# A planned order that knows of a port VectorE and GpSimd share, with new ranks and costs, and two buffers swapped in the last stage

## The chip, the cores and the metric

The kernel runs on one core of a Trainium2 chip. Its time is the device time of one execution in microseconds (us). Before the change three runs took 959.69, 960.66 and 961.48 us; the median, 960.66, is the number that counts. The engines are called by their short names: PE is TensorE, DVE is VectorE, ACT is ScalarE, POOL is GpSimd, SP is SyncE, which here issues nearly all DMAs.

## What is computed

The reference is causal attention with a decay, followed by two gated layers:

```python
cum = np.cumsum(np.log(np.clip(f, 0.0001, 1.0)), axis=-1)
scores = np.matmul(q, k.transpose(0, 1, 3, 2)) / sqrt(64) + (cum[..., :, None] - cum[..., None, :])
attn = softmax(where(causal, -1e9, scores))            # 4 batches, 8 heads, 576 tokens, head size 64
x = (attn @ v), heads laid side by side                # 2304 tokens x 512
h = x @ w_in                                           # 512 -> 2048
x = (h * sigmoid(h)) @ w_out                           # 2048 -> 512
out = ((x @ w_a) * (x @ w_b)) @ w_out2                 # 512 -> 1536 -> 512
```

## The kernel before

The work runs in five stages, one behind the other on PE, with their edges interleaved. (1) Attention, in 16 pairs of heads: scores `s` into PSUM (L453), on DVE a scaled copy that also gives the row minimum (L479), on ACT the exponential with a row sum (L487), on PE transposes of the weights `p` into the banks `t_x` and `t_y` (L529), copies of those to SBUF as `th` (L534, on ACT or DVE), and the product with `v` into `pv` (L575). (2) The first gated layer into 2048 columns (`job`, L729 for the products). (3) Its way out (`out_first`, L935). (4) The second gated layer into 1536 (`job` again). (5) Its way out (`out_pairs`, L1083).

The matrix products of stages 2 to 5 are done with seven products instead of eight per 2 x 2 block, so sums and differences of quarters have to be formed first (`combine`), and every fp32 operand is split in two parts, `hi` (a cast on ACT, L619) and `lo` (value minus `hi`, L620), so that three matmuls stand for one. The `lo` part and the sums run on DVE or POOL. `either` lets the planner choose between the two, `ss` fixes DVE, `pool` fixes POOL. `make_forms` makes the seven forms of the activations (`x`, `xa`, `xb`), `load_unit` those of a unit of weights (`w`), from words that `decode` unpacks (on ACT L679 and L680, on DVE L681 and L682). Buffers go in turns: the weights of unit n lie in `wA`, `wB` or `wC`, by n modulo 3, and what a later stage puts there waits for the last product that reads the unit.

The order on every engine is not written by hand. Each piece of work is handed to `Plan.add` with an engine, a cost in ns, what it reads and writes and a rank (`prio`, lower first). `Plan.order` plays the pieces through with those costs: of the candidates of the engine that can start soonest it takes the lowest rank among those startable within 30 ns, and the instructions are then issued in the order of the planned starts. So a cost that is off does not change what is computed, only who stands ahead of whom in an engine's queue. Before, a DVE piece marked `port` that overlapped a busy POOL was charged 0.9 of the overlap more, and POOL nothing.

## Time and profile before

| | |
|---|---|
| median of the three runs | 960.66 us |
| the profiled execution | 959.04 us, span 957.3 us, granted clock 1.00 |
| PE busy | 931.6 us (97%) |
| DVE busy | 702.2 us (73%) |
| ACT busy | 610.7 us (64%) |
| POOL busy | 369.3 us (39%) |
| PE's share of the chain that ended last | 79% |

All numbers of the profile come from that one execution; its own time is 1.6 us below the median. A row of a timeline gives start, length, engine, line, operation, what it writes and reads, how many instructions are merged in it, and in brackets the idle time of the engine ahead of it and who ended that. Line numbers in rows are those of the kernel before.

### The profile page before, as it was taken

To read this page: it belongs to the slowest core of one execution; us is meant where nothing else is said; L and a number is where in the kernel's file an instruction comes from. 1 tells how busy PE (TensorE), PEld (TensorE's weight loads), DVE (VectorE), ACT (ScalarE), POOL (GpSimd) and SP (SyncE) were. 2 spreads that over 40 slices of the span, in tenths; PEclk is the share of its full clock that TensorE was granted. 3 is DMA by queue.
4 is the path that set the end of the run, shared out by engine and by line. 5 is a ranking of instruction groups with operands and counts; after the bars stand their busy time and mean duration, and the time that the engine had idled before them with its cause. 6 is when DMAs were issued, how large, how long until landed. Compare 5 with 4: busy or idle time off the path is not lost.

```text
span 957.3 us, 16537 instructions
## 1 busy us (share of the span) xinstructions
PE 931.6 (97%) x5892; PEld 875.3 (91%) x5892; DVE 702.2 (73%) x1293; ACT 610.7 (64%) x1186; POOL 369.3 (39%) x341
## 2 busy tenths in 40 slices
PE   8999999999999999999999889999999999999998
PEld 7666666799999999999999789999999999999997
DVE  7776898776756587798559987675655668977874
ACT  5999989975678885556444656675555534553642
POOL 5466576000465211463015783633444447400000
PEclk9999999999999999999999999999999999999999
DMA  5543553337566599768758406555555325896861
GB/s 156 178 161 128 155 178 100 106 117 266 202 249 244 201 357 402 283 205 314 281 195 286 149 1 241 172 200 192 199 188 185 129 102 192 288 321 236 277 213 67
DMA packets 79074, 194.24 MB, mean 203 GB/s; under 512 B 11020, under 2 KB 36764, under 8 KB 78960
## 3 DMA queue, kind: packets, MB, share of 16 engines
q1 hardware_dynamic: 78880, 192.74, 58.1%
q8 instruction: 46, 0.75, 0.3%
q10 hardware_dynamic: 112, 0.45, 0.2%
q14 instruction: 36, 0.29, 0.1%
HBM read 126.31 MB, written 66.84 MB: 202 GB/s over the span
## 4 chain that ended last, share of the span: by engine, by line
PE 79%; ACT 7%; DVE 5%; issue 4%; DMA 2%; POOL 2%; SPq 1%; DVEq 0%; ACTq 0%; POOLq 0%
PE a L729 22%; PE m L1083 13%; PE b L729 11%; PE f L935 10%; PE d L935 7%; PE g L729 6%; PE s L453 3%; PE pv L575 2%; ACT raw L680 1%; PE t_y L529 1%; ACT p L487 1%; PE t_x L529 1%; ACT th L534 1%; DMA rb<-invs 1%; POOL w L620 1%
## 5 line engine op out<-in xcount | busy, mean ns | idle before, releaser
L729 PE MATMUL a<-x,w 128*128 128x384 f32 x960 | 185.1, 335 | 0.7 <-DVE d L802 0.7
L620 POOL TENSOR_TENSOR w<-m,w 128x512 fp32r<-128x512 f32 x80 | 99.7, 1255 | 206.7 <-ACT w L619 206.7
L729 PEld LDWEIGHTS a<-x,w 128*128 128x128 f32 x960 | 167.7, 188 | 1.6 <-DVE d L802 1.0
L729 PE MATMUL b<-x,w 128*128 128x384 f32 x480 | 96.6, 335 | 3.9 <-POOL w L620 2.1
L680 ACT ACTIVATE raw<-raw 128x512 uint16<-128x512 uint16 x68 | 91.1, 1388 | 0.6
L729 PEld LDWEIGHTS b<-x,w 128*128 128x128 f32 x480 | 84.1, 188 | 4.8 <-POOL w L620 2.4
L487 ACT ACTIVATE p<-p,nm 128x512 f32<-128x512 f32 (+3 forms) x128 | 70.8, 563 | 3.9 <-DVE nm L479 3.9
L729 PE MATMUL a<-xb,w 128*128 128x384 f32 x360 | 71.2, 334 | 0.9 <-ACT c L787 0.9
L1083 PE MATMUL m<-morea,wo 128*128 128x384 f32 x378 | 68.1, 334 | 0.7 <-DVE morea L620 0.7
L1083 PEld LDWEIGHTS m<-morea,wo 128*128 128x128 f32 x378 | 65.7, 188 | 1.0 <-DVE morea L620 1.0
L619 ACT CAST w<-m 128x512 fp32r<-128x512 f32 x80 | 44.1, 571 | 32.9 <-POOL m L703 21.6
L729 PEld LDWEIGHTS a<-xb,w 128*128 128x128 f32 x360 | 63.1, 188 | 1.2 <-ACT c L787 1.2
L479 DVE CUSTOM_DVE_ANT_0 p<-s,maskw 128x512 f32<-128x512 f32 (+3 forms) x128 | 56.4, 482 | 8.2 <-PE s L453 2.7
L405 POOL TENSOR_TENSOR qkl<-qk,qkh 128x304 fp32r<-128x304 f32 x60 | 51.7, 891 | 27.1 <-DVE qkh L397 26.0
L682 DVE SCALAR_TENSOR_TENSOR m<-raw,m 128x512 uint32<-128x512 uint32 x56 | 45.0, 808 | 18.0 <-ACT raw L680 17.6
L802 DVE TENSOR_TENSOR d<-a,c 128x384 f32<-128x384 f32 x60 | 33.7, 561 | 28.8 <-PE a L729 27.6
L784 ACT COPY c<-b 128x384 f32<-128x384 f32 x60 | 29.1, 487 | 35.9 <-PE b L729 35.8
L729 PE MATMUL g<-x,w 128*128 128x384 f32 x240 | 48.1, 335 | 0.4 <-ACT c L763 0.4
L787 ACT COPY c<-a 128x384 f32<-128x384 f32 x60 | 29.6, 493 | 29.5 <-PE a L729 29.3
L779 ACT COPY c<-a 128x384 f32<-128x384 f32 x60 | 29.3, 488 | 29.8 <-PE a L729 27.8
L729 PE MATMUL b<-xa,w 128*128 128x384 f32 x240 | 48.0, 334 | 0.0
L575 PE MATMUL pv<-th,vt 128*64 128x448 f32 (+4 forms) x384 | 46.8, 393 | 0.0
(233 smaller groups left out, 2282.7 us busy)
## 6 DMA issues: line engine op xcount, KB each, us to landing
raw<-in_w SPq DMA_DIRECT2D x68, 512.0 KB
cdram<-z SPq DMA_DIRECT2D x36, 576.0 KB
g<-gdram SPq DMA_DIRECT2D x24, 768.0 KB
c_False<-cdram SPq DMA_DIRECT2D x36, 384.0 KB
c_True<-cdram SPq DMA_DIRECT2D x36, 384.0 KB
gdram<-z SPq DMA_DIRECT2D x32, 384.0 KB
h<-gdram SPq DMA_DIRECT2D x16, 576.0 KB
qk<-in_qk SPq DMA_DIRECT2D x15, 608.0 KB
```

The source lines that it names most:

```text
L405: plan.add("POOL", t_pool(QK // 4), lambda c=c: nc.gpsimd.tensor_sub(lo()[:, c], raw()[:, c], hi().bitcast(F32)[:, c]), [(hi, "h"), raw], ...
L479: plan.add("DVE", t_dve(nj) + 82, lambda out=out, low=low, o=o, mk=mk: nc.vector.tensor_tensor_reduce(out(), o(), mk, -SCALE, 3.0e38, ALU. ...
L487: plan.add("ACT", t_act(sum(IB[ib]), 279), lambda b=b, c=c, nj=sum(IB[ib]): nc.scalar.activation(b()[:, :nj], b()[:, :nj], AF.Exp, bias=nm ...
L575: nc.tensor.matmul(ps()[p * D:(p + 1) * D, o0:o0 + w_].rearrange("d (u c) -> d u c", c=D), vt()[:, jb, p], src, start=n == 0, stop=last)
L619: act(n, lambda: nc.scalar.copy(hi(), val()), reads, [key + (0,)], pr)
L620: eng(n, lambda e: e.tensor_sub(lo(), val(), hi().bitcast(F32)), list(reads) + [key + (0,)], [key + (1,)], pr)
L680: act(n, lambda: nc.scalar.activation(short(2), short(1), AF.Relu, bias=7.0, scale=-2.0 ** -13), [], [raw], pr)
L682: plan.add("DVE", 690, lambda: nc.vector.scalar_tensor_tensor(bits(), high(), 0x80000007, bits(), ALU.bitwise_and, ALU.bitwise_xor), [raw] ...
L729: nc.tensor.matmul(ps()[:, :HB], a, b, start=start and k == 0 and i == 0, stop=k == 1 and i == 2, skip_group_check=not start)
L802: dve(HB, lambda e: e.tensor_add(pd(), pa(), pc(2)), [a, (c, 2)], [d], at(4) - 3)
L935: nc.tensor.matmul(ps[o]()[:, :HB], a, b, start=start and i == 0, stop=stop and i == 2, skip_group_check=not fresh)
L1083: nc.tensor.matmul(ps[o]()[:, :HB], a, b, start=start and i == 0, stop=stop and i == 2, skip_group_check=not fresh)
```

## The change

Costs, ranks and one pair of buffers change; what is computed does not. In the planner: a DVE piece with `port` and a POOL piece that overlap now slow each other (DVE to 0.55, POOL to 0.7 of its speed), and the other's planned end is moved too; an engine is taken to be free 40 to 100 ns before a piece ends; a wait on the own engine costs 25 ns. Costs: the exponential 118 ns more, the copy of transposes to 163 ns plus length, the second unpacking step on ACT 1290 ns, POOL 2.17 ns a column. Ranks: exponentials later (now behind the copies of transposes, which come earlier), the multiplication by the inverse sums later; the forms of the second gated layer 7 to 12 us later for two groups and 20 us earlier for one. In the last stage `few`, the first buffer of split operands, goes to `wA` and `saved` to `wB`, and the first operands rank further ahead.

```diff
     SWITCH, STAY = 150, 0.9
+    DRAIN = {"DVE": 80, "ACT": 100, "POOL": 40}
+    SHARED = {"DVE": 0.55, "POOL": 0.7}
...
+        port = {}
+        def contend(eng, op, start, dur):
+            other = port.get("POOL" if eng == "DVE" else "DVE")
+            if other is None or (eng == "DVE" and not op.port):
+                return dur, 0, None
+            mine, theirs = self.SHARED[eng], self.SHARED[other.eng]
+            begin, end = max(start, other.start), other.start + other.dur
+            if begin >= end or begin >= start + dur:
+                return dur, 0, None
+            left, rest = end - begin, dur - (begin - start)
+            both = min(rest / mine, left / theirs)
+            return dur + both * (1 - mine), both * (1 - theirs), other
...
-                            e + (0 if eng == way[0] == "PE" else self.LATENCY[eng]) for eng, e in known[op].items()))
-                        if way[0] == "DVE" and op.port:
-                            way = ("DVE", way[1] + 0.9 * min(way[1], max(0, free.get("POOL", 0) - start)), way[2])
+                            e + (0 if eng == way[0] == "PE" else 25 if eng == way[0] else self.LATENCY[eng]) for eng, e in known[op].items()))
+                        if way[0] in self.SHARED:
+                            way = (way[0], contend(way[0], op, start, way[1])[0], way[2])
...
-            free[op.eng] = t + op.dur
+            free[op.eng] = t + op.dur - self.DRAIN.get(op.eng, 0)
...
+                if more:
+                    other.dur, other.end = other.dur + more, other.end + more
+                    free[other.eng] += more
...
-    return 133 + 2.5 * n
+    return 133 + 2.17 * n
...
-    PRIO = dict(s=-2.2, max=-2.3, exp=-1.5, t=-1.3, cp=-0.85, pv=1.5, fin=-0.3, dec=2, load=-5.3)
+    PRIO = dict(s=-2.2, max=-2.3, exp=-0.93, t=-1.3, cp=-0.99, pv=1.5, fin=-0.03, dec=2, load=-5.3)
...
-            plan.add("ACT", t_act(sum(IB[ib]), 279), lambda b=b, c=c, nj=sum(IB[ib]): nc.scalar.activation(
+            plan.add("ACT", t_act(sum(IB[ib]), 397), lambda b=b, c=c, nj=sum(IB[ib]): nc.scalar.activation(
...
-        plan.add("POOL", 250 + 2.65 * n, lambda: fn(nc.gpsimd), reads, writes, prio)
+        plan.add("POOL", 180 + 2.17 * n, lambda: fn(nc.gpsimd), reads, writes, prio)
...
-        act(n, lambda: nc.scalar.activation(short(2), short(1), AF.Relu, bias=7.0, scale=-2.0 ** -13), [], [raw], pr)
+        plan.add("ACT", 1290, lambda: nc.scalar.activation(short(2), short(1), AF.Relu, bias=7.0, scale=-2.0 ** -13), (), [raw], pr)
...
-        saved = buf(None, "wA", [P, 4, 2, HB], F32, "saved")
-        few = buf(None, "wB", [P, 1, 2, 4, HB], F32R, "few")
+        saved = buf(None, "wB", [P, 4, 2, HB], F32, "saved")
+        few = buf(None, "wA", [P, 1, 2, 4, HB], F32R, "few")
...
+            ahead = 14 if not (g or second or v) else 6
...
-            make_forms(1, 0, 0, 1000 + t + 36)
+            make_forms(1, 0, 0, 1000 + t + 16)
...
-    make_forms(1, 1, 1, 1000 + t - 10)
-    make_forms(1, 2, 2, 1000 + t)
+    make_forms(1, 1, 1, 1000 + t - 3)
+    make_forms(1, 2, 2, 1000 + t + 12)
```

The number of instructions hardly moves: POOL has 352 instead of 346, DVE 1274 instead of 1279, ACT 1046 instead of 1047, SP 589 in both; PE has 20 fewer matmuls on `idle`, which only fill planned gaps in the first 40 us. Where they stand moves, at three places that matter here.

On PE in attention, around the product of pair 6 (`pv_6`): `s_7_1` are the scores of pair 7's first two blocks, `s_8_4` those of pair 8's last block, `t_7_x0` and `t_7_x1` transposes of pair 7. Before:

```order
826 L529 MATMUL t_7_x0_1519<-ident_77,p_7_None_4_1454 128x128
827 L529 MATMUL t_7_x1_1521<-ident_77,p_7_None_4_1454 128x128
828 L575 MATMUL pv_6_1_1526<-th_6_0_1381,vt_6_1291 64x448 x2
829 L575 MATMUL pv_6_1_1526<-th_6_1_1438,vt_6_1291 64x448 x2
830 L575 MATMUL pv_6_1_1526<-th_6_2_1442,vt_6_1291 64x320 x2
831 L575 MATMUL pv_6_1_1526<-th_6_3_1466,vt_6_1291 64x192 x2
832 L575 MATMUL pv_6_1_1526<-th_6_3_1466,vt_6_1291 64x64 x2
833 L575 MATMUL pv_6_0_1537<-th_6_2_1442,vt_6_1291 64x128 x2
834 L453 LDWEIGHTS decay0_108
835 L453 MATMUL s_7_1_0_1552<-decay0_108 128x256
```

The same place in the changed kernel:

```order
814 L480 MATMUL s_8_4_1_1528<-qkl_8_1371,qkh_8_1352 128x288
815 L480 MATMUL s_8_4_1_1528<-qkh_8_1352,qkl_8_1371 128x288
816 L556 MATMUL t_7_x0_1540<-ident_77,p_7_None_4_1391 128x128
817 L556 MATMUL t_7_x1_1543<-ident_77,p_7_None_4_1391 128x128
818 L556 MATMUL t_7_x0_1540<-ident_77,p_7_0_3_1464 128x2x64
819 L556 MATMUL t_7_x1_1543<-ident_77,p_7_0_3_1464 128x2x64
820 L556 MATMUL t_7_x0_1540<-ident_77,p_7_1_3_1477 128x2x64
821 L556 MATMUL t_7_x1_1543<-ident_77,p_7_1_3_1477 128x2x64
822 L602 MATMUL pv_6_1_1557<-th_6_0_1369,vt_6_1269 64x448 x2
```

Pair 6's product now stands behind the rest of pair 7's scores, pair 8's first scores and the whole of the transposes into `t_7_x0` and `t_7_x1`.

On POOL where the second gated layer begins: `w_1_1` is its second unit of weights, made out of the pieces `m_34` and `m_35`; `x_1_2` are the forms of the third group of tokens, which PE reads last; `xb_1_1` belongs to the second group. Before:

```order
158 L620 TENSOR_TENSOR xb_1_1_6451<-z0_1_1_6149,xb_1_1_6451 128x768 x2
159 L620 TENSOR_TENSOR w_1_1_6560<-m_34_6408,w_1_1_6560 128x512
160 L620 TENSOR_TENSOR w_1_1_6560<-m_35_6417,w_1_1_6560 128x256
161 L703 TENSOR_TENSOR m_35_6417<-m_35_6417 128x256
162 L620 TENSOR_TENSOR x_1_2_6584<-z1_1_2_6290,x_1_2_6584 128x768
163 L703 TENSOR_TENSOR m_35_6417<-m_34_6408,m_35_6417 128x256
164 L620 TENSOR_TENSOR x_1_2_6584<-z0_1_2_6262,x_1_2_6584 128x768
165 L703 TENSOR_TENSOR m_34_6408<-m_35_6417,m_34_6408 128x256
166 L620 TENSOR_TENSOR w_1_1_6560<-m_35_6417,w_1_1_6560 128x512
```

The same place in the changed kernel:

```order
158 L647 TENSOR_TENSOR xb_1_1_6437<-z0_1_1_6130,xb_1_1_6437 128x768 x2
159 L647 TENSOR_TENSOR xb_1_1_6437<-z1_1_1_6145,xb_1_1_6437 128x768
160 L647 TENSOR_TENSOR w_1_1_6524<-m_34_6385,w_1_1_6524 128x512
161 L647 TENSOR_TENSOR w_1_1_6524<-m_35_6391,w_1_1_6524 128x256
162 L730 TENSOR_TENSOR m_35_6391<-m_35_6391 128x256
163 L730 TENSOR_TENSOR m_35_6391<-m_34_6385,m_35_6391 128x256
164 L730 TENSOR_TENSOR m_34_6385<-m_35_6391,m_34_6385 128x256
165 L730 TENSOR_TENSOR m_34_6385<-m_34_6385 128x256
166 L647 TENSOR_TENSOR w_1_1_6524<-m_35_6391,w_1_1_6524 128x512
167 L647 TENSOR_TENSOR w_1_1_6524<-m_34_6385,w_1_1_6524 128x512
168 L647 TENSOR_TENSOR x_1_2_6557<-z0_1_2_6225,x_1_2_6557 128x768
```

The unit's work now stands in one piece, with one more split for `xb_1_1` (from DVE) ahead of it; of the three `x_1_2` splits one is left on POOL, behind it, and two are on DVE.

On DVE where the last stage begins, `few` being the first split operands of that stage, `c_0_False_0` what they come from, `wo_1_1` weights for its later products. Before:

```order
1094 L1106 TENSOR_TENSOR d_0_False_0_9029<-c_0_False_0_8934 128x768
1095 L802 TENSOR_TENSOR d1_10_1_9044<-a1_10_1_8922,c1_10_1_8943 128x384
1096 L809 TENSOR_TENSOR z1_10_1_9052<-c1_10_1_8943,d1_10_1_9044 128x384
1097 L818 TENSOR_TENSOR c1_10_1_8943<-g1_10_1_9035,c1_10_1_8943 128x384
1098 L856 TENSOR_TENSOR m_1_5_9008<-m_1_5_9008 128x256
1099 L620 TENSOR_TENSOR wo_1_1_8917<-m_1_5_9008,wo_1_1_8917 128x512
1100 L830 TENSOR_TENSOR z1_10_1_9052<-c1_10_1_8943,a1_10_1_8922 128x384
1101 L620 TENSOR_TENSOR wo_1_1_8917<-m_1_5_9008,wo_1_1_8917 128x512
1102 L620 TENSOR_TENSOR few_9074<-c_0_False_0_8934,few_9074 128x768
1103 L620 TENSOR_TENSOR few_9074<-d_0_False_0_9029,few_9074 128x768
```

The same place in the changed kernel:

```order
1093 L1134 TENSOR_TENSOR d_0_False_0_9002<-c_0_False_0_8920 128x768
1094 L647 TENSOR_TENSOR few_8979<-c_0_False_0_8920,few_8979 128x768
1095 L829 TENSOR_TENSOR d1_10_1_9033<-a1_10_1_8903,c1_10_1_8922 128x384
1096 L647 TENSOR_TENSOR few_8979<-d_0_False_0_9002,few_8979 128x768
1097 L836 TENSOR_TENSOR z1_10_1_9054<-c1_10_1_8922,d1_10_1_9033 128x384
1098 L845 TENSOR_TENSOR c1_10_1_8922<-g1_10_1_9016,c1_10_1_8922 128x384
1099 L824 TENSOR_TENSOR c1_11_1_9000<-b1_11_1_9005,c1_11_1_9000 128x384
1100 L857 TENSOR_TENSOR z1_10_1_9054<-c1_10_1_8922,a1_10_1_8903 128x384
1101 L647 TENSOR_TENSOR wo_1_1_8897<-m_1_5_8988,wo_1_1_8897 128x512
```

The two splits of `few` moved up by six places, and one of the two `wo_1_1` splits and the sum of `m_1_5` between them went to POOL. On PE the first product that reads `few` now stands two products earlier.

## Rows read from the trace of the kernel before

**Rows 1.** Windows: stretch, its length, busy PE, PEld, DVE, ACT, POOL; clock, DMA.

```profile
20.00:195.00 175.00, 169.33 (x1453) 120.39 (x1453) 137.72 (x461) 161.34 (x425) 90.89 (x91) 1.00 0.43 141
195.00:310.00 115.00, 112.85 (x648) 111.89 (x647) 75.48 (x113) 80.27 (x158) 37.78 (x36) 1.00 0.61 220
310.00:510.00 200.00, 200.00 (x1155) 199.94 (x1154) 145.20 (x187) 122.83 (x202) 56.20 (x46) 1.00 0.78 280
510.00:546.00 36.00, 31.22 (x174) 29.56 (x173) 35.96 (x37) 21.56 (x33) 22.95 (x14) 1.00 0.70 231
546.00:580.00 34.00, 30.32 (x171) 29.14 (x170) 30.00 (x39) 18.87 (x32) 26.43 (x14) 1.00 0.11 37
...
810.00:830.00 20.00, 18.27 (x104) 17.63 (x103) 19.04 (x24) 10.89 (x17) 13.30 (x11) 1.00 0.83 273
```

**Rows 2.** Groups of instructions of ACT in 20 to 195 us, costliest first.

```profile
L487 ACT ACTIVATE p<-p,nm 128x512 f32<-128x512 f32 (+3 forms) x120 | 66.4, 564 | 0.8 <-DVE nm L479 0.8
L534 ACT COPY th<-t_x 128x384 f32<-128x384 f32 (+1 forms) x58 | 28.8, 524 | 9.0 <-PE t_x L529 8.6
...
L680 ACT ACTIVATE raw<-raw 128x512 uint16<-128x512 uint16 x10 | 13.5, 1377 | 0.0
```

**Rows 3.** Timeline of ACT, then of PE, 87 to 97 us.

```profile
92.73 0.87 ACT L534 COPY th<-t_x 128x384 f32<-128x384 f32 x2 [1.09 <-PE t_x L529]
...
88.32 2.92 PE L575 MATMUL pv<-th,vt 128*64 128x448 f32 x24
```

**Rows 4.** Timeline of ACT at 253 us and of PE at 256 us.

```profile
253.72 2.51 ACT L680 ACTIVATE raw<-raw 128x512 uint16<-128x512 uint16 x2
...
256.60 1.33 PE L729 MATMUL b<-x,w 128*128 128x384 f32 x6 [0.86 <-ACT c L784]
```

**Rows 5.** Timeline of POOL, then of DVE, from 500 us on.

```profile
500.08 6.69 POOL L620 TENSOR_TENSOR x<-z,x 128x768 fp32r<-128x768 f32 x3 [57.76 <-DMA sdram<-t]
...
500.33 4.74 DVE L620 TENSOR_TENSOR wo_1b<-h,wo_1b 128x768 fp32r<-128x768 f32 x2
...
507.98 0.94 DVE L639 TENSOR_TENSOR z<-z,z 128x768 f32<-128x768 f32 x1
```

**Rows 6.** Timeline of POOL up to and while `w_1_1` is made, 546 to 569 us.

```profile
546.12 6.44 POOL L620 TENSOR_TENSOR xb<-z,xb 128x768 fp32r<-128x768 f32 x1 [4.78 <-ACT xb L619]
...
555.36 1.99 POOL L620 TENSOR_TENSOR w<-m,w 128x512 fp32r<-128x512 f32 x2 [2.80 <-ACT w L619]
...
558.75 2.54 POOL L620 TENSOR_TENSOR x<-z,x 128x768 fp32r<-128x768 f32 x1
...
562.67 2.54 POOL L620 TENSOR_TENSOR x<-z,x 128x768 fp32r<-128x768 f32 x1
...
566.58 1.98 POOL L620 TENSOR_TENSOR w<-m,w 128x512 fp32r<-128x512 f32 x1
```

**Rows 7.** Timeline of PE in the same stretch.

```profile
552.34 2.24 PE L935 MATMUL f<-hl_B,wo 128*128 128x384 f32 x12
...
565.99 0.52 PE L729 MATMUL b<-x,w 128*128 128x384 f32 x2
568.61 0.96 PE L729 MATMUL b<-x,w 128*128 128x384 f32 x4 [2.10 <-POOL w L620]
```

**Rows 8.** Timeline of PE, then of DVE, 810 to 824 us.

```profile
816.04 1.20 PE L729 MATMUL a<-xb,w 128*128 128x384 f32 x6
...
819.52 2.18 PE L1083 MATMUL m<-few,wo 128*128 128x384 f32 x11 [1.06 <-DVE few L620]
...
823.59 2.20 PE L1083 MATMUL m<-morea,wo 128*128 128x384 f32 x11 [0.68 <-DVE morea L620]
...
810.01 1.49 DVE L1106 TENSOR_TENSOR d_False<-c_False 128x768 f32<-128x768 f32 x1
...
816.27 1.78 DVE L620 TENSOR_TENSOR few<-c_False,few 128x768 fp32r<-128x768 f32 x1
817.98 1.48 DVE L620 TENSOR_TENSOR few<-d_False,few 128x768 fp32r<-128x768 f32 x1
```

More of the change, by code (lines that the diff above doesn't have):

```diff
@@ L193, in order @@
             op.start, op.end = t, t + op.dur + op.after
-            free[op.eng] = t + op.dur
+            free[op.eng] = t + op.dur - self.DRAIN.get(op.eng, 0)
+            if op.eng in self.SHARED and (op.eng == "POOL" or op.port):
+                base = next(w[1] for w in op.ways if w[0] == op.eng)
+                _, more, other = contend(op.eng, op, t, base)
+                port[op.eng] = op
+                if more:
+                    other.dur, other.end = other.dur + more, other.end + more
+                    free[other.eng] += more
+                    for u in users[other]:
+                        if u.start is None:
+                            known[u][other.eng] = max(known[u].get(other.eng, 0), other.end)
             ready.remove(op)
@@ L533, in transpose @@
             col += P if shared else 2 * P
-        eng = [("ACT", t_act(col) + 30, lambda: nc.scalar.copy(out(), ps()[:, :col])),
+        eng = [("ACT", t_act(col, 163), lambda: nc.scalar.copy(out(), ps()[:, :col])),
                ("DVE", t_dve(col) + 80, lambda: nc.vector.tensor_copy(out(), ps()[:, :col]))]
@@ L607, in pool @@
     def pool(n, fn, reads, writes, prio):
-        plan.add("POOL", 250 + 2.65 * n, lambda: fn(nc.gpsimd), reads, writes, prio)
+        plan.add("POOL", 180 + 2.17 * n, lambda: fn(nc.gpsimd), reads, writes, prio)
     def either(n, fn, reads, writes, prio):
-        plan.add("POOL", 250 + 2.65 * n, lambda: fn(nc.gpsimd), reads, writes, prio,
+        plan.add("POOL", 180 + 2.17 * n, lambda: fn(nc.gpsimd), reads, writes, prio,
                  also=[("DVE", 100 + n / 0.88, lambda: fn(nc.vector))], port=True)
@@ L1102, in pair @@
             if second:
-                ss(HB, lambda e: e.tensor_add(tmp()[:, 0], raw()[:, 0], raw()[:, 3]), rk, [tmp], p - 6)
+                ss(HB, lambda e: e.tensor_add(tmp()[:, 0], raw()[:, 0], raw()[:, 3]), rk, [tmp], p - ahead)
                 sets = ((2, 2, lambda: raw()[:, 1:3], rk), (1, 1, lambda: tmp()[:, :1], [tmp]))
             else:
-                ss(2 * HB, lambda e: e.tensor_sub(flat(tmp()[:, :2]), flat(raw()[:, :2]), flat(raw()[:, 2:])), rk, [tmp], p - 6)
+                ss(2 * HB, lambda e: e.tensor_sub(flat(tmp()[:, :2]), flat(raw()[:, :2]), flat(raw()[:, 2:])), rk, [tmp], p - ahead)
                 sets = ((0, 2, lambda: raw()[:, ::3], rk), (2, 2, lambda: tmp()[:, :2], [tmp]))
@@ L1109, in pair @@
             for c, (_, n, val, reads) in enumerate(sets):
-                split(n * HB, lambda at=at, n=n: x()[:, 0, at:at + n], lambda at=at, n=n: x()[:, 1, at:at + n], val, reads, key + (c,), p - 5, ss)
+                split(n * HB, lambda at=at, n=n: x()[:, 0, at:at + n], lambda at=at, n=n: x()[:, 1, at:at + n], val, reads, key + (c,), p + 1 - ahead, ss)
                 at += n
```

## The prediction

> **What bounds the kernel now.** I read the windows first. Each number behind a duration is busy time, and the brackets count the matmuls [rows 1]. From 310 to 510 us PE is busy in all 200 us with 1155 matmuls, so one matmul of the usual shape costs 200 / 1155 = 0.1732 us and nothing is lost. With that price the other stretches give their loss as length minus count times price: 195 to 310 us 115 − 648 × 0.1732 = 2.8 us; 510 to 546 us 36 − 174 × 0.1732 = 5.9; 546 to 580 us 34 − 171 × 0.1732 = 4.4; 810 to 830 us 20 − 104 × 0.1732 = 2.0. These 15.1 us are most of what a better order can win behind attention. Attention, 20 to 195 us, is another kind of stretch: PE is busy 169.3 of 175 us there, with matmuls of many shapes, and ACT 161.3 of 175. Neither is full; each waits for the other now and then, and ACT's idle time is 175 − 161.3 = 13.7 us. The groups of ACT then say for what: 9.0 us of it stand ahead of the copies `th`, 8.6 of them waiting for PE's transposes `t_x` [rows 2]. The timelines name the waits in the other stretches [rows 4 to 8].
>
> **Attention.** The change adds 118 ns to the planned exponential, of which 120 run here at 564 ns [rows 2], so the old plan had ACT done some 120 × 0.118 = 14 us too early over the stage and put `pv` products ahead of transposes as if ACT were served. An example: `pv` holds PE for 2.92 us at 88.32 and ends at 91.24; ACT's copy at 92.73 had waited 1.09 us for the transposes behind it [rows 3]. In the new order the scores and transposes of the next pair stand ahead of `pv`. What it is worth can't be read from a row. The end of gain is all of ACT's idle time, 13.7 us; the end of loss is one more such wait of 1.09 us in each of 15 pairs, 16.4 us, if the later rank of the exponentials leaves the transposes without weights. I take a third of the 8.6 us, 3 us of gain, since the direction is that of the largest wait, but `pv` still has to run somewhere, and PE itself has only 175 − 169.3 = 5.7 us free.
>
> **Decoding on ACT, 195 to 310 us.** The second unpacking step is planned at 1290 ns instead of less than half of it; it takes 1377 [rows 2]. ACT runs two in a row, 2.51 us from 253.72 to 256.23, and the copy `c<-b` that stands behind them in ACT's queue keeps PE 0.86 us at 256.60 [rows 4]; the same happens once more 51 us later. Each such stop also costs PE a restart: the stretch lost 2.8 us, against about 1.7 us of idle time for the two. Planned at their length, the two steps no longer stand ahead of a copy that is due, so I take 2.0 us of the 2.8. Bounds: 0, if they merely block another copy, and 2.8.
>
> **Forms for the second layer, 500 to 546 us.** POOL makes three splits `x` in 6.69 us while DVE makes two splits of the same 768 columns in 4.74; alone, DVE needs 0.94 for one [rows 5]. So the two do not run side by side: 6.69 is about three POOL shares of (6.69 − 2 × 0.94) / 3 = 1.60 with DVE's between them. One of the `x` splits goes to DVE, which takes 1.60 from POOL's run and puts 0.94 into DVE's: `wo_1b` and `hl_C` behind them come 0.7 us earlier. The stops of PE that follow remain, so of the 5.9 us I take 0.7 (0 to 1.6).
>
> The Trainium skill says of this in "SBUF — State Buffer", section "Who interferes with whom", that the shared pair of ports is an exclusive lock for a whole instruction and that the loser is fully blocked and not throttled. The trace agrees with turns: a DVE split of 0.94 us takes 2.37 beside POOL [rows 5]. The new planner instead lets both run on at 0.55 and 0.7, together 1.25, so its overlaps come out too cheap; by the page's rule DVE's share would go wholly into the waiting of one of the two, which is rival C.
>
> **`w_1_1`, 546 to 580 us.** POOL works on it from 555.36 to 566.58 + 1.98 = 568.56, 13.2 us, with two `x` splits of 2.54 between [rows 6]; PE has begun the product `b` at 565.99 and stops 2.10 us for it [rows 7]. In the new order these splits stand behind the unit or on DVE: 13.2 − 2 × 2.54 = 8.1 us. One `xb` split more stands ahead, about 2.54 us, but POOL was idle 2.80 us there, waiting for a cast of ACT [rows 6], so it fits, unless DVE stretches it. The unit is then ready at 555.36 + 8.1 = 563.5, or up to 0.8 us earlier if PE's gains upstream bring ACT's cast forward. PE comes earlier too: its `hl_B` products stand two products ahead of their old place, and counted from 552.34 [rows 7] nine products of 6 × 0.1732 = 1.04 us stand ahead of the `b` that waited, so PE arrives at 561.7. A wait of 1.0 to 1.8 us is left instead of the loss of 4.4, which also had stops on ACT and DVE behind it in the queue: gain 3.2 us, bounds 0 and 4.4. Behind the waiting product on PE nothing else can pass, so what is left is paid in full. Late next are the `x` splits of the third group of tokens, which PE reads last.
>
> **`few`, 810 to 830 us.** DVE makes the two splits at 816.27 and 817.98, and PE stops 1.06 us at 819.52 for them, then 0.68 at 823.59 for `morea` [rows 8]. The change puts the splits six places up, right behind `d_False`, which ends at 810.01 + 1.49 = 811.50. With both splits (1.78 and 1.48) and one 384-column sum of about half an 0.94 us split between them, `few` stands at about 815.2. PE reads it two products earlier than before, at 816.04 [rows 8], so this wait is gone. For this `few` lies in `wA`, free sooner than `wB`; the source `c_False` is already there, since DVE reads it at 810.01, so no DMA decides. The wait for `morea` stays in part, 0.4 us. Gain 2.0 − 0.4 = 1.6. Bounds: 2.0, and −1.5, the length of one split, if the last unit in `wA` is read so long that the first split waits.
>
> **What costs nothing or is new.** POOL gets six instructions more and DVE five fewer; POOL is busy 56 of 200 us in the long middle stretch [rows 1], which hides them. The 20 idle matmuls of PE fill gaps only. SP issues the same 589 DMAs; the loads for `x_1_2` stand two places earlier, past raw weights that are due later. A newly made order also makes new stops: I put in two of the kind that rows show, 0.68 [rows 8] and 0.86 [rows 4], 1.5 us, with none and eight of them, 0 and 6, as the ends.
>
> **The sum.** −3.0 − 2.0 − 0.7 − 3.2 − 1.6 + 1.5 = −9.0. The profiled execution took 959.04 us, so 950.0; it lies 1.6 us below the median of the three runs, 960.66, so the forecast on that is 951.6.
>
> **The rivals.**
>
> A, the forecast: 946 to 957, chance 0.55.
>
> B, attention gives more: with exponentials and copies planned at their real length ACT's queue never stands behind PE, and two thirds of its 13.7 us go, 9 instead of 3. 951.6 − 6 = 945.6. For it: 8.6 of the 13.7 us have one cause [rows 2]. Against it: PE has just 5.7 us of free time there, so 9 need PE's own work to be shorter, by waits inside its busy time. Chance 0.15.
>
> C, the port works by turns: what the order moved from POOL to DVE blocks POOL as long as it runs, the `xb` split ahead of `w_1_1` takes 6.44 us, as the one at 546.12 did [rows 6], rather than 2.54, and the gains of `w_1_1` and `few` are given back. 951.6 + 3.2 + 1.6 = 956.4. For it: 6.69 and 4.74 us [rows 5]. Against it: only one split more lies ahead of the unit. Chance 0.12, a quarter of it within the bound of no change.
>
> D, the stops only move: the order differs, PE stops as often elsewhere. 960.7. Chance 0.08.
>
> E, slower: the exponentials now rank behind the copies, so ACT copies while PE's next transposes wait for weights. The price is one wait of 1.09 us [rows 3] in each of 15 pairs, 16.4 us, in place of the gain of 3: 951.6 + 3.0 + 16.4 = 971.0. It decides from (960.66 − 954.6) / 15 = 0.4 us a pair. For it: ACT has the least room of all engines but PE in attention; against it: the copies it is ranked behind are what PE's `pv` needs anyway. Chance 0.10.
>
> **The numbers.** Below about 0.2%, 1.9 us, a measurement of this kernel can't be told from no change. Faster: 0.55 of A, 0.15 of B and 0.09 of C, 0.79. Same: D with the rest of C, 0.11. Slower: E, 0.10. The range takes A and C whole, most of D's near side and half of B, and leaves E out: 943 to 959.5.
>
> **What the profile after would show.** Attention is right if ACT's idle time ahead of `th` falls from 9.0 to about 6 us, and E is right if PE's transposes wait for the exponentials. The decoding term is right if no `b` product between 195 and 310 us waits for a copy. `w_1_1` is right if POOL makes it in about 8 us without a break and PE's wait for it is below 2 us; C is right if the split ahead of it takes over 4 us. `few` is right if PE's first product of the last stage doesn't wait. The forecast is wrong if new stops beyond 3 us appear in the stretch from 310 to 510 us, where there are none, or if the first layer starts later than before.

## The result and the profile after

The changed kernel takes 945.0 us (median of six runs, 944.36 to 946.56) against 960.96 of the kernel before in the same comparison (six runs, 959.35 to 963.41). The ratio is 0.9836, 95% interval 0.9820 to 0.9852: 16 us faster. 951.6 was forecast. The time lies inside the range, but 1 us below the band of the forecast itself (A, 946 to 957) and almost on rival B's 945.6; whether B's mechanism was at work is taken up below. The profiled execution took 944.4 us with a span of 942.7, against 957.3 before: 14.6 us less, where the sum had 9.0. The other 1.4 us are the places of the two profiled executions in their samples.

The windows of the kernel after, with the columns of [rows 1], cut at about the same places of the work:

```profile
20.00:182.00 162.00, 159.70 (x1387) 112.79 (x1386) 126.51 (x452) 152.67 (x417) 94.33 (x93) 1.00 0.46 151
...
195.00:300.00 105.00, 104.93 (x606) 104.61 (x605) 69.28 (x102) 74.07 (x145) 39.42 (x36) 1.00 0.61 221
300.00:500.00 200.00, 199.95 (x1154) 199.63 (x1153) 143.59 (x181) 122.25 (x203) 63.33 (x53) 1.00 0.80 285
500.00:532.00 32.00, 29.76 (x167) 28.45 (x166) 31.96 (x33) 19.90 (x32) 20.05 (x13) 1.00 0.68 223
532.00:570.00 38.00, 36.80 (x209) 35.83 (x208) 37.16 (x49) 22.24 (x37) 23.62 (x18) 1.00 0.24 89
...
800.00:815.00 15.00, 14.58 (x84) 14.06 (x83) 13.40 (x19) 6.71 (x12) 12.37 (x10) 1.00 0.79 263
```

The same sum as before the change, length minus count times 0.1732 us, gives the losses now; the matmuls from 570 to 800 us lose nothing.

| stretch | lost before | lost after | change | forecast |
|---|---|---|---|---|
| behind attention, to 310 (300) us | 2.8 | 0.0 | −2.8 | −2.0 |
| the long middle, to 510 (500) us | 0.0 | 0.1 | +0.1 | |
| between the layers, to 580 (570) us | 5.9 + 4.4 | 3.1 + 1.8 | −5.4 | −0.7 − 3.2 |
| the last stage begins | 2.0 | 0.4 | −1.6 | −1.6 |
| new stops | | | in the rows above | +1.5 |
| attention: what is left of 14.6 | | | −4.9 | −3.0 |

Every gain has the forecast sign, and all but the last stage's came out larger; the new stops stayed away. The split between attention and what follows is good to about half a us: matmul 100 of the first layer (counted from 0) begins at 197.31 us instead of 203.22, 5.9 us earlier, of which some 0.5 is a stop of PE at 196 us that the table has in its first row. In attention the last `pv` product starts at 183.20 us instead of 190.09; six matmuls of the first layer that stood ahead of it (1.0 us) moved behind it, so that not all of the 6.9 us is a gain. What PE's transposes wait for in attention shows where it came from (groups of PE, 20 to 182 us, first before, then after):

```profile
L529 PE MATMUL t_y<-ident,p 128*128 128x128 f32 x180 | 27.0, 282 | 3.3 <-ACT th L534 3.0
L529 PE MATMUL t_x<-ident,p 128*128 128x128 f32 x122 | 22.9, 278 | 1.8 <-DVE th L535 1.7
```

```profile
L556 PE MATMUL t_y<-ident,p 128*128 128x128 f32 x192 | 28.2, 279 | 0.4 <-ACT th L561 0.2
...
L556 PE MATMUL t_x<-ident,p_None 128*128 128x128 f32 x75 | 17.4, 292 | 0.8 <-ACT th L561 0.8
```

With 0.3 us on a third group before, PE waited 5.0 us for the copies `th` that make its banks free, and 1.0 us after. The groups of ACT, 20 to 195 us, with the columns of [rows 2]:

```profile
L514 ACT ACTIVATE p<-p,nm 128x256 f32<-128x256 f32 (+3 forms) x123 | 67.7, 558 | 0.9 <-DVE nm L506 0.8
L561 ACT COPY th<-t_x 128x384 f32<-128x384 f32 (+1 forms) x53 | 26.2, 512 | 5.7 <-PE t_x L556 5.7
...
L707 ACT ACTIVATE raw<-raw 128x512 uint16<-128x512 uint16 x11 | 15.1, 1368 | 0.0
```

ACT's idle time ahead of `th` fell from 9.0 to 5.7 us, as forecast, though the experiments show that this idle time is a poor measure. Between the layers, the timelines of POOL and then PE at `w_1_1`, against [rows 6, 7]:

```profile
543.15 1.86 POOL L647 TENSOR_TENSOR xb<-z,xb 128x768 fp32r<-128x768 f32 x1 [1.76 <-ACT xb L646]
544.96 1.99 POOL L647 TENSOR_TENSOR w<-m,w 128x512 fp32r<-128x512 f32 x2
...
552.15 3.26 POOL L647 TENSOR_TENSOR w<-m,w 128x512 fp32r<-128x512 f32 x2
...
553.08 1.37 PE L756 MATMUL b<-x,w 128*128 128x384 f32 x6
```

The extra `xb` split took 1.86 us, and the unit started right behind it without a wait for ACT. The first of its last two splits, half of 3.26 us, ended near 553.8, 8.8 us after the start (8.1 forecast). PE's `b` took 1.37 us where six matmuls otherwise show 1.20, so of the 2.10 us of waiting some 0.2 is left, not 1.0 to 1.8. The stops on `wo_1b` and `hl_B` remain, as forecast, but shorter, and one on `hl_C` went (timeline of PE, first after, then before):

```profile
527.29 2.18 PE L962 MATMUL f<-wo_1b,wo 128*128 128x384 f32 x11 [1.32 <-DVE wo_1b L647]
...
535.13 1.15 PE L962 MATMUL f<-hl_B,wo 128*128 128x384 f32 x5 [1.19 <-DVE hl_B L647]
```

```profile
534.39 2.20 PE L935 MATMUL f<-wo_1b,wo 128*128 128x384 f32 x11 [1.73 <-DVE wo_1b L620]
...
539.04 2.18 PE L935 MATMUL f<-hl_C,wo 128*128 128x384 f32 x11 [1.20 <-DVE hl_C L620]
...
543.02 3.24 PE L935 MATMUL f<-hl_B,wo 128*128 128x384 f32 x17 [1.62 <-DVE hl_B L620]
```

With a shorter stop on `hl_C` in each (0.23 us at 525.10 before, 0.88 at 518.39 after), these stops came to 4.8 us before and 3.4 after.

At the last stage, DVE and then PE, against [rows 8]:

```profile
799.34 0.95 DVE L647 TENSOR_TENSOR few<-c_False,few 128x768 fp32r<-128x768 f32 x1
800.67 1.03 DVE L647 TENSOR_TENSOR few<-d_False,few 128x768 fp32r<-128x768 f32 x1
...
803.03 1.20 PE L1110 MATMUL m<-few,wo 128*128 128x384 f32 x6
...
810.03 2.18 PE L1110 MATMUL m<-morea,wo 128*128 128x384 f32 x11 [0.42 <-DVE morea L647]
```

`few` is ready at 801.70, 1.3 us before PE reads it, and the wait for `morea` is 0.42 us (0.4 forecast). The splits are also shorter, 0.95 and 1.03 us instead of 1.78 and 1.48.

### The profile page after: what moved, and what is told of

It reads as the page before. It is cut to its first block, busy times and chain, and to the rows that moved or that the text cites. A ratio compares the mean times of both kernels' runs of the same rounds, so it can differ in the third digit from the quotient of the medians.

```text
span 942.7 us, 16499 instructions
## 1 busy us (share of the span) xinstructions
PE 928.6 (99%) x5872; PEld 874.2 (93%) x5872; DVE 700.8 (74%) x1288; ACT 609.3 (65%) x1185; POOL 370.5 (39%) x347
## 4 chain that ended last, share of the span: by engine, by line
PE 54%; DVE 4%; DMA 1%; issue 1%; POOL 1%; ACT 0%; DVEq 0%; POOLq 0%; SPq 0%
PE a L756 15%; PE m L1110 13%; PE f L962 8%; PE b L756 7%; PE d L962 7%; PE g L756 4%; DVE z L666 1%; DMA sdram<-t 1%; DVE hl_C L647 1%; DVE wo_1b L647 1%; DVE hl_B L647 1%; DMA h<-gdram 0%; POOL m L883 0%; DMA m<-wdram 0%; POOL wo L647 0%
## 5 line engine op out<-in xcount | busy, mean ns | idle before, releaser
L806 ACT COPY c<-a 128x384 f32<-128x384 f32 x60 | 29.5, 491 | 41.3 <-PE a L756 38.9
L709 DVE SCALAR_TENSOR_TENSOR m<-raw,m 128x512 uint32<-128x512 uint32 x56 | 41.5, 746 | 11.1 <-ACT raw L707 10.5
L883 POOL TENSOR_TENSOR m<-m 128x256 f32<-128x256 f32 x40 | 39.5, 1006 | 14.3 <-DMA m<-wdram 12.5
```

Of the source, the lines that this page charges most:

```text
L709: plan.add("DVE", 690, lambda: nc.vector.scalar_tensor_tensor(bits(), high(), 0x80000007, bits(), ALU.bitwise_and, ALU.bitwise_xor), [raw] ...
L883: either(2 * P, lambda e: (e.tensor_add if add else e.tensor_sub)(m()[:, o], m()[:, a], m()[:, b]), [keys[a], keys[b]], [keys[o]], p)
```

## The experiments

All are timed against the kernel before, in three rounds. The first three columns of numbers are results; the others are read from PE's timeline: the start of the last `pv` product, and the time from matmul 858 of the first way out to matmul 1099 of the layers' products (counted from 0), "between". In the expectations matmul 2355 of the layers' products and 94 of the last stage are counted alike. The kernel before took 960.49, 959.34 and 960.56 us in the three rounds, so a difference between kernels of two rounds is good to about 1.6 us. The six matmuls of the first layer (1.0 us) stand ahead of the last `pv` in all rows but after, after − ACT costs, − forms' ranks, − buffers and after, short step.

| kernel | median us | ratio to before | interval | last pv | between |
|---|---|---|---|---|---|
| before | 960.96 | | | 190.09 | 60.9 |
| after | 945.00 | 0.9836 | 0.9820 to 0.9852 | 183.20 | 55.6 |
| before + unpacking cost | 960.50 | 1.0001 | 0.9990 to 1.0012 | 185.25 | 64.1 |
| before + exponential's cost | 956.50 | 0.9954 | 0.9938 to 0.9970 | 187.23 | 60.8 |
| before + ranks | 959.47 | 0.9989 | 0.9979 to 0.9999 | 189.67 | 61.3 |
| after − ACT costs | 962.76 | 1.0023 | 1.0014 to 1.0033 | 196.03 | 54.4 |
| after − forms' ranks | 951.38 | 0.9913 | 0.9896 to 0.9930 | 184.31 | 61.3 |
| after − port rule | 965.96 | 1.0065 | 1.0042 to 1.0088 | 189.97 | 63.3 |
| after − buffers | 948.29 | 0.9879 | 0.9860 to 0.9897 | 183.21 | 57.7 |
| after − unpacking cost | 955.86 | 0.9963 | 0.9945 to 0.9980 | 189.54 | 54.4 |
| before, short step | 953.23 | 0.9931 | 0.9912 to 0.9949 | 186.90 | 60.9 |
| after, short step | 945.86 | 0.9852 | 0.9835 to 0.9869 | 182.89 | 55.6 |
| after, step at 1377 | 952.23 | 0.9916 | 0.9900 to 0.9932 | 190.61 | 56.0 |
| after, port in turns | 948.89 | 0.9881 | 0.9866 to 0.9896 | 187.53 | 53.7 |

**Which number carries attention?** First, single parts on the kernel before.

```diff
-        act(n, lambda: nc.scalar.activation(short(2), short(1), AF.Relu, ...
+        plan.add("ACT", 1290, lambda: nc.scalar.activation(short(2), short(1), AF.Relu, ...
```

> The kernel before with one number of the change: the second unpacking step planned at 1290 ns. In the traces the last pv product starts at 190.09 us before and at 183.20 after, and the product jobs stand 7.9 us earlier after 325 us. Theory (the exponential's cost carries attention, the unpacking cost only the two waits between 195 and 310 us): pv ends within 1 us of 190, the b waits at 256 and 307 us go, time 2 us below before. Rival (the ten unpacking steps that also run inside attention, each planned 0.76 us short, carry most of it): the last pv starts at 186 or earlier, time 5 to 8 us below before.

The last `pv` came 4.8 us earlier, as the rival said of attention, and against my theory, that this cost mattered only behind attention. On the time both missed: it stayed the same. Some 2 us were given back behind attention and 3.2 between the layers, where PE stopped 3.06 us for `hl_B` and the granted clock read 0.75 in the 4 us from 540 us on. Timelines of ACT and PE of that kernel, near 300 us:

```profile
301.00 2.49 ACT L680 ACTIVATE raw<-raw 128x512 uint16<-128x512 uint16 x2
...
303.81 0.48 ACT L784 COPY c<-b 128x384 f32<-128x384 f32 x1
...
304.34 1.31 PE L729 MATMUL b<-x,w 128*128 128x384 f32 x6 [2.46 <-ACT c L784]
```

Two steps stand ahead of a copy that PE waits for, as before, although the plan now knows their length.

```diff
-            plan.add("ACT", t_act(sum(IB[ib]), 279), lambda b=b, c=c, ...
+            plan.add("ACT", t_act(sum(IB[ib]), 397), lambda b=b, c=c, ...
```

> The kernel before with one number of the change: the exponential planned 118 ns longer. Theory: the last pv product starts near 184.5 us (most of the 6.9 us), ACT's idle time ahead of the th copies falls from 9.0 to about 6 us, time 5 to 6 us below before. Rival (unpacking cost or ranks carry it): last pv within 2 us of 190, time within 2 us of before.

Neither: 2.9 us at the last `pv`, 4.0 in all. And the marker that I had chosen fails (groups of ACT, 20 to 182 us):

```profile
L534 ACT COPY th<-t_x 128x384 f32<-128x384 f32 (+1 forms) x48 | 24.1, 520 | 16.2 <-PE t_x L529 16.2
```

ACT is idle 16.2 us ahead of `th`, more than before, in a kernel that is faster: with fewer copies on ACT (48 and not 57 in that window) it has slack, and its idle time is no measure of what PE loses. The kernel after with the short step (below) has 9.3 us of it, as much as before, and is as fast as after.

```diff
-    PRIO = dict(..., exp=-1.5, t=-1.3, cp=-0.85, pv=1.5, fin=-0.3, ...
+    PRIO = dict(..., exp=-0.93, t=-1.3, cp=-0.99, pv=1.5, fin=-0.03, ...
```

> The kernel before with the new ranks of exponentials, copies and inverse sums alone, costs as before. Theory: without the longer costs the later rank of the exponentials is worth nothing by itself, last pv between 188 and 192 us, time within 2 us of before. Rival E of the prediction (late exponentials starve the transposes): last pv later than 195 us, time 5 us or more above before. Rival (ranks carry attention's gain): last pv at 185 or earlier, time 5 us or more below before.

As the theory said: nothing of attention's gain, and no starving: the last `pv` is at 189.67 us. Then all three ACT costs taken out of the kernel after:

```diff
-            plan.add("ACT", t_act(sum(IB[ib]), 397), lambda b=b, c=c, ...
+            plan.add("ACT", t_act(sum(IB[ib]), 279), lambda b=b, c=c, ...
...
-        eng = [("ACT", t_act(col, 163), lambda: nc.scalar.copy(out(), ps()[:, :col])),
+        eng = [("ACT", t_act(col) + 30, lambda: nc.scalar.copy(out(), ps()[:, :col])),
...
-        plan.add("ACT", 1290, lambda: nc.scalar.activation(short(2), short(1), AF.Relu, ...
+        act(n, lambda: nc.scalar.activation(short(2), short(1), AF.Relu, ...
```

> The kernel after without its three ACT costs (exponential, copy of transposes, second unpacking step go back), ranks and port kept. Theory: attention's gain is given back, last pv near 189 us instead of 183.20, and the waits of b for c return between 190 and 310 us: time 7 to 9 us above after. Rival (ranks or the port's planning carry attention): last pv within 2 us of 183, time 2 to 3 us above after.

Attention gave back 12.8 us, more than the whole gain: the last `pv` at 196.03. The time is 17.8 us above after, twice the forecast; another 6.4 us were lost behind attention, where PE waited 1.31, 0.53 and 1.97 us for copies of ACT and the granted clock read 0.60 for the 4 us after the last of these. In attention PE waits for ACT's copies (groups of PE, 20 to 182 us, to be compared with those of the result):

```profile
L556 PE MATMUL t_y<-ident,p 128*128 128x128 f32 x180 | 26.3, 280 | 4.3 <-ACT th L561 4.0
...
L556 PE MATMUL t_x<-ident,p_None 128*128 128x128 f32 x70 | 18.1, 307 | 4.2 <-ACT th L561 3.8
```

These waits come to 7.8 us, against 5.0 before and 1.0 after. So the rest of the change under a plan that takes ACT for faster than it is does starve PE. It is not rival E: what PE waits for are the copies that free its banks, not the exponentials, and the late ranks alone, at the same old costs, did not do it. The gain between the layers stays, 54.4 us.

```diff
-        plan.add("ACT", 1290, lambda: nc.scalar.activation(short(2), short(1), AF.Relu, ...
+        act(n, lambda: nc.scalar.activation(short(2), short(1), AF.Relu, ...
```

> The kernel after with the second unpacking step planned at 617 ns again, the exponential's and the copies' longer costs kept. With one number changed on the kernel before, the unpacking cost brought the last pv 4.8 us forward and the exponential's 2.9. Theory (both say the same to the planner, that ACT is fuller than it thinks, and don't add): last pv at 185 to 187 us, 2 to 4 us later than after; a wait of b for c of 0.5 us or more is back between 195 and 310 us; time 3 to 5 us above after. Rival (the unpacking cost alone carries attention): last pv at 188 us or later, time 6 us or more above after. Rival (the exponential's cost suffices with the ranks): last pv within 1 us of 183.20.

This alone costs the kernel after 10.9 us, 6.3 of them at the last `pv` (5.3 without the six matmuls), as the rival said, and PE's waits for ACT between 195 and 310 us are back: 1.65, 0.55 and 1.99 us. The ACT cost that I had booked at 2 us, behind attention only, moves more than that. How much of it is this cost and how much the order that comes with any other number is the question of the runs that follow.

**Is it the lag or the order?** The next two keep each kernel's order, and shorten the step on the chip instead of lengthening it in the plan.

```diff
-        ... nc.scalar.activation(short(2), short(1), AF.Relu, ...
+        ... nc.scalar.activation(short(2)[:, :176], short(1)[:, :176], AF.Relu, ...
```

> The kernel before, in the same order on every engine, with the second unpacking step run on 176 of its 512 columns (the other columns of the weights are not unpacked), so that it lasts about as long as its plan of 617 ns says. Theory (what hurt in attention was ACT running behind its plan): some ten steps are 0.76 us shorter each, the last pv product comes 4 to 7 us earlier, 183 to 186 us, and the b waits at 256 and 307 us are gone; time 5 to 9 us below before. Rival (the order itself, not ACT's lag): last pv within 2 us of 190, time within 3 us of before.

> The kernel after, in the same order on every engine, with the same shortening of the step. It now lasts half of the planned 1290 ns. Theory (after's order already has room for the step): the last pv comes at most 2 us earlier than 183.20, the rest of the kernel as after; time 0 to 2 us below after, well under what the shortening gives before. Rival (the shortening simply takes work from a full ACT): last pv 4 us or more earlier, as much as before gains.

The step's row in the groups of ACT, 20 to 182 us, first of before shortened, then of after shortened:

```profile
L680 ACT ACTIVATE raw<-raw 128x176 uint16<-128x176 uint16 x9 | 5.2, 611 | 0.0
```

```profile
L707 ACT ACTIVATE raw<-raw 128x176 uint16<-128x176 uint16 x9 | 5.4, 598 | 0.0
```

The step lasts 611 ns, what the old plan of 617 assumed. Before gains 7.3 us by it: 3.2 at the last `pv`, short of the 4 to 7 forecast, and 2.4 more up to 350 us, where the `b` waits at 256 and 307 us are gone. In attention it is the wait for ACT's copies that shrinks, from 3.0 to 0.5 us (group of PE in before shortened, 20 to 182 us):

```profile
L529 PE MATMUL t_y<-ident,p 128*128 128x128 f32 x192 | 27.5, 279 | 0.7 <-ACT th L534 0.5
```

After gains nothing at the median (945.86 against 945.0) and 0.3 us at the last `pv`, though the same work left ACT. So the length of the step costs before's order 7.3 us and after's order nothing. The likely reading is that what costs before's order is not the length but its being unplanned, since that order was made for 617 ns. A shortening of another, rightly planned operation of ACT, which would separate the two, was not tried.

**The parts of the rest.**

```diff
-            make_forms(1, 0, 0, 1000 + t + 16)
+            make_forms(1, 0, 0, 1000 + t + 36)
-    make_forms(1, 1, 1, 1000 + t - 3)
-    make_forms(1, 2, 2, 1000 + t + 12)
+    make_forms(1, 1, 1, 1000 + t - 10)
+    make_forms(1, 2, 2, 1000 + t)
```

> The kernel after with the three old ranks of the second layer's forms. From the first out stage's product number 858 to the second layer's job product 1099 the kernel before takes 60.9 us, the kernel after 55.6. Theory (the forms' ranks keep the x splits out of w_1_1's way on POOL): 3 to 4 us of the 5.4 come back, 59 us or more, PE stops again over 1.5 us for w_1_1; time 3 us above after. Rival (the port's planning does it, whatever the ranks): 56.5 us or less, time within 1 us of after.

The stretch is back at 61.3 us, all of the 5.4 and a little more (the time 6.4 us above after, where 3 were forecast), and PE waits for `w_1_1` (PE, then POOL):

```profile
563.21 0.98 PE L756 MATMUL a<-x,w 128*128 128x384 f32 x4 [1.54 <-POOL w L647]
...
550.02 2.71 POOL L647 TENSOR_TENSOR w<-m,w 128x512 fp32r<-128x512 f32 x2 [14.26 <-ACT w L646]
...
561.07 2.08 POOL L647 TENSOR_TENSOR w<-m,w 128x512 fp32r<-128x512 f32 x1 [0.73 <-ACT w L646]
```

POOL is idle 14.26 us ahead of the unit here, waiting for ACT's cast, and there is no `x` split inside it. So the ranks carry the stretch, but not, in this order, by the splits that I had counted; what makes ACT's cast late stays open. The gain does not hang on one order, either: with the old ranks of the forms the stretch takes 60.8 to 64.1 us in all five orders of the table, with the new ones and a two-sided port rule 53.7 to 57.7 in all six.

```diff
-                        if way[0] in self.SHARED:
-                            way = (way[0], contend(way[0], op, start, way[1])[0], way[2])
+                        if way[0] == "DVE" and op.port:
+                            way = ("DVE", way[1] + 0.9 * min(way[1], max(0, free.get("POOL", 0) - start)), way[2])
...
-            if op.eng in self.SHARED and (op.eng == "POOL" or op.port):
+            if False:
```

> The kernel after with the old rule for the port: a DVE piece that overlaps a busy POOL is charged 0.9 of the overlap, POOL nothing. Theory (forms' ranks carry the stretch between the stages, ACT costs attention): last pv within 1.5 us of 183.20, the stretch from out product 858 to job product 1099 within 1.5 us of 55.6, time 0 to 2 us above after. Rival (the two-sided rule carries it): the stretch at 58 us or more, time 4 us or more above after.

The largest miss: 21 us above after, and slower than before, as the rival said. The last `pv` is 6.8 us later than in after (5.8 without the six matmuls), the stretch between the layers takes 63.3 us, 7.8 more, and the rest is spread over the other stages. The clock has a part in it at two places. In attention PE waits 2.42 us for DVE up to 118.64, and the granted clock is 0.50 from 120 to 124 us. Between the layers it falls after this stop (timeline of PE, and windows with the columns of [rows 1]):

```profile
544.82 3.89 PE L962 MATMUL f<-hl_C,wo 128*128 128x384 f32 x11 [3.46 <-DVE hl_C L647]
```

```profile
545.00:555.00 10.00, 10.00 (x45) 10.00 (x46) 9.27 (x12) 4.39 (x6) 5.88 (x2) 0.76 0.46 164
```

In these 10 us PE is busy throughout and does 45 matmuls instead of 10 / 0.1732 = 58. How much of the 21 us the rule itself costs, and how much the stops that this one order happens to have, is open.

```diff
-        saved = buf(None, "wB", [P, 4, 2, HB], F32, "saved")
-        few = buf(None, "wA", [P, 1, 2, 4, HB], F32R, "few")
+        saved = buf(None, "wA", [P, 4, 2, HB], F32, "saved")
+        few = buf(None, "wB", [P, 1, 2, 4, HB], F32R, "few")
...
-            ahead = 14 if not (g or second or v) else 6
+            ahead = 6
```

> The kernel after with few in wB, saved in wA and the first operands ranked as before. From job product 2355 to product 94 of the last stage before takes 47.2 us, after 45.8. Theory: PE waits again about 1 us for few and the stretch takes 47.2, all else unchanged, time 1.4 us above after. Rival (the earlier planned DVE and POOL pieces bring few in time in either buffer): within 0.3 us of 45.8, time as after.

The wait for `few` is back, longer than before (PE, then DVE), and that stretch takes 48.1 us. Another 2.1 us were lost between the layers, where only the order changed: PE waited 2.26 us for `hl_B` instead of 1.19, and the granted clock read 0.71 from 540 to 544 us.

```profile
809.01 2.18 PE L1110 MATMUL m<-few,wo 128*128 128x384 f32 x11 [1.92 <-DVE few L647]
...
805.80 1.76 DVE L647 TENSOR_TENSOR few<-c_False,few 128x768 fp32r<-128x768 f32 x1
807.48 1.48 DVE L647 TENSOR_TENSOR few<-d_False,few 128x768 fp32r<-128x768 f32 x1
```

**How much of it is the particular order?**

```diff
-        plan.add("ACT", 1290, lambda: ...
+        plan.add("ACT", 1377, lambda: ...
```

> The kernel after with the step planned at the 1377 ns that it takes in the trace of before, instead of 1290. Theory (costs near the measured ones are what help): time within 2 us of after, last pv within 1 us of 183.20. Rival (after is one lucky order among many that the planner gives for nearly the same costs): the stretches move by several us either way, time 3 us or more above after.

The rival holds. With the measured cost in the plan the kernel is 7.2 us slower than after, all of it by the last `pv`, at 190.61 us. The `pv` of pair 8 starts at 108.0 us, ahead of after's 108.6; that of pair 9 at 125.1 against 120.4. Between them (windows, then PE, DVE and POOL):

```profile
113.00:117.00 4.00, 2.41 (x20) 1.67 (x19) 4.00 (x6) 3.64 (x6) 4.00 (x3) 1.00 0.58 170
117.00:121.00 4.00, 2.55 (x22) 1.82 (x21) 4.00 (x13) 1.79 (x5) 1.27 (x1) 0.81 0.23 92
121.00:125.00 4.00, 4.00 (x21) 3.41 (x19) 3.68 (x19) 1.22 (x5) 3.23 (x4) 0.50 0.07 13
```

```profile
116.94 0.77 PE L480 MATMUL s<-decay 64*128 64x384 bf16 x2 [1.59 <-DVE p_None L502]
...
112.63 2.19 DVE L672 CAST x<-z 128x768 fp32r<-128x768 f32 x1
114.74 1.79 DVE L522 TENSOR_SCALAR sm<-sm 128x9 f32<-128x9 f32 x1
...
111.85 6.42 POOL L673 TENSOR_TENSOR x<-z,x 128x768 fp32r<-128x768 f32 x3
```

On DVE a cast of 768 columns takes 2.19 us and an operation on nine columns 1.79 us while POOL runs three splits without a break. PE, which was busy 2.41 and 2.55 us of two windows of 4 us, stops for 1.59 and 0.98 us in them, and its clock reads 0.50, the lower of its two levels, in the next 4 us. That the overlap with POOL is what stretched the two DVE operations is read from the times alone.

This bears on all that was said of single numbers: 87 ns more on the same cost move the last `pv` by 7.4 us (6.4 without the six matmuls), as much as any other change of one number did.

```diff
-    SHARED = {"DVE": 0.55, "POOL": 0.7}
+    SHARED = {"DVE": 0.5, "POOL": 0.5}
```

> The kernel after with both speeds of the port rule at 0.5, so that two overlapping pieces cost as much as one behind the other. Theory (the traces show turns, so the rule that sums to one is nearer to the chip): the stretch from out product 858 to job product 1099 at 55.6 us or less, time 0 to 3 us below after. Rival (the rates 0.55 and 0.7 suit this order and nothing else): time 3 us or more above after, most of it in other stretches.

Both in part: the stretch between the layers is the shortest of all, 53.7 us, but attention ends 4.3 us later than after (3.3 without the six matmuls), and the kernel is 3.9 us slower than after, where 0 to 3 us faster was forecast. No version measured beats after.

## Why the prediction was right, and where its sizes were off

**Direction and range** were right because the bound was read right: behind attention the time is PE's matmuls at 0.1732 us plus what they wait, and the waits named in [rows 4, 7 and 8] went or shrank. That the time came out at rival B's 945.6 is chance: B wanted 9 us from attention, which gave about 5. Of the 5.6 us beyond the forecast 3.7 came from elsewhere: decoding (0.8), the stretch between the layers (1.5) and the new stops that stayed away (1.4).

**Attention** was sized at a third of 8.6 us, −3.0; it gave −4.9 by the table. The mis-sizing has two parts. The step that said the exponential made the old plan wrong named one cause of two: the unpacking steps inside attention, too, ran 0.76 us longer than planned, and with the order held they cost 3.2 us at the last `pv`. Which of the two weighs more the single edits can't say, since 87 ns moved as much. And the size was taken from the wrong engine: ACT's idle time says little, as two of the runs show; PE's own says more. It fell from 5.7 to 2.3 us, with the waits for the copies `th` down from 5.0 to 1.0; the other 1.5 us of the gain came out of PE's busy time. So rival B's main objection, PE's small room, held. E did not come: what after's transposes still wait for are copies, 1.0 us, and not exponentials.

**Decoding** came to −2.8 (2.0 forecast). With the order held, the shortened step removed both waits, so the step's full length made them; the correct cost by itself did not keep them away (2.46 us at 304 us), so here I had nearly the right sum from a plan that is more than that cost.

**Between the layers**, −0.7 − 3.2 became −5.4. The forms' ranks carry it, together with the new port rule; that they do so by the `x` splits on POOL, as the steps had it, is what after's order shows and the order with the old ranks does not. Two terms were too small. The wait left over at `w_1_1` was 0.2 us and not 1.0 to 1.8: the unit took 8.8 us, 0.7 more than forecast, but it started without its 2.80 us of waiting for ACT's cast, of which only up to 0.8 us had been granted. And the stops on `wo_1b`, `hl_C` and `hl_B` gave 1.4 us instead of 0.7. The 0.94 us for a DVE split alone was read from a row that is a sum of the same shape (`z<-z,z`, [rows 5]); the splits of `few` in after, 0.95 and 1.03 us, bear it out.

**`few`** was right in its size and its rows. **New stops**, +1.5, were overestimated: the long middle lost 0.1 us and no other stop of the size assumed appeared.

**Rival C** did not happen in this order, for the `xb` split took 1.86 us and not 6.44. That DVE's work beside a busy POOL can cost PE as much is what the order planned at 1377 ns shows, where 5.3 us are lost between two `pv` products, part of them through the clock. D is excluded by the table.

What stays open is how far each part earns its gain by being truer. Taken out one by one, the parts cost 3.3, 6.4, 10.9 and 21.0 us, together far over 16, and a truer number (1377) costs 7.2. The parts do not add, and in three of these five orders the clock fell on top; after is one good order among neighbours, of which the two measured lie 3.9 and 7.2 us above it. What is shown with the order held fixed is that the 0.76 us by which the step outran its plan cost before's order 7.3 us in all and that after's order has room for the step; what is shown over many orders is the forms' ranks with the port rule, between the layers. That these particular rates and ranks are right is not shown, and POOL's shorter costs, the engines taken to be free 40 to 100 ns early and the 25 ns for a wait on the own engine were never taken out by themselves.

## What to carry to other kernels

Where a planner sets the order, compare each planned length with the trace first, and look at the error of one step as well as at the sum: here the step that was off by 0.76 us ran ten times in attention and cost 3.2 us there, with the order held. To tell a wrong plan from a full engine, hold the order and shorten the operation to its planned length: if the time falls in the old order and not in the new one, it speaks for the plan. And judge a single planner number with several neighbours, since a change of 87 ns moved this kernel by 7 us.

## What had not been expected of the hardware

Stops of PE of a few us cost more than their length where the clock falls after them: 0.50 for 4 us after 1.59 and 0.98 us of waiting, 0.76 on the mean of 10 us after 3.46 us. Before and after show 1.00 in every window given here, with stops of 2.10 us [rows 7], so not every such stop does it. The same stop shows both: before + ranks waits 2.12 us for `w_1_1`, the kernel before 2.10, at nearly the same place in a stretch with the same stops, and the granted clock of 568 to 572 us is 0.73 in the one and 1.00 in the other, with PE busy 2.54 and 2.69 of these 4 us. The clock fell so in six of the ten orders that the experiments made, which is part of why neighbouring plans lie several us apart. And a DVE operation on nine columns took 1.79 us beside a busy POOL, where its mean in attention is 0.41 us in the kernel after:

```profile
L522 DVE TENSOR_SCALAR sm<-sm 128x9 f32<-128x9 f32 x16 | 6.6, 414 | 9.8 <-ACT p L514 9.8
```
